# Two of 64 cache-gradient stores, issued in three parts by two queues

## The chip, the cores and the metric

The kernel runs on one core of one Trainium2 chip. The metric is device time in microseconds of one launch. A run's time is a little longer than the span of the profile, which goes from the first to the last instruction of the program.

## What is computed

The reference is one decode step of an attention block and a gated MLP that stand side by side, and its whole backward pass. Only the core of it is shown; everything is bfloat16, with a batch of 2, one query position, 32 query heads over 16 key heads, a cache of 4096 positions and a head size of 128.

```python
q = (xn @ wq) per head;  k, v = caches, each shared by 2 query heads
o = softmax(q k^T / sqrt(128)) v;  y_attention = o @ wo
h = (xn @ w_gate) * (xn @ w_up);   y_mlp = h @ w_down
out = x + y_attention + y_mlp                        # xn = layernorm(x)
_out, _vjp = jax.vjp(_f, A_x, A_k_cache, A_v_cache, A_wq, A_wo, B_w_gate, B_w_up, B_w_down)
_grads = _vjp(grad_out)
return (_out0, *[jnp.asarray(_g) for _g in _grads])
```

The two caches and their gradients make up most of the bytes. A cache has 2 x 16 slabs of 4096 x 128 elements (1 MB each), and its gradient has as many. Since there is one query position, the gradient of a slab is an outer product: of the softmax weights with the head's output gradient for V, and of the score gradients with the query for K.

## The kernel before

**Steps.** The kernel walks through 16 steps `s`. Each takes one batch entry `b` and one group `g` of two key heads, so it loads four slabs: K and V for `l` = 0 and 1. `t` = 0 stands for K and `t` = 1 for V. A slab lies in SBUF as 128 rows of 32 positions, 8192 bytes a row. A step turns the slabs with VectorE transposes (`turn`), forms scores on TensorE (`score`), the softmax, the output and the score gradients, and then the two cache gradients.

**The gradients of the caches.** GpSimd builds a block-diagonal matrix `BD` of the query or of the output gradient (`build_BD`) and copies small weight tiles `W` (`build_W`). `outer` waits for `BD` and starts a `head_outer` for each of the two heads. That one takes one of the store buffers `st`, which share sixteen 8 KB-a-row tiles called `big` with the caches and other work (at most five of them may be store buffers). It has four units of work; a unit is a pair of matmuls into PSUM and an eviction by ScalarE or VectorE into a quarter of the buffer. When all four are in, `put` stores the buffer as a slab of `out_2` or `out_3`, one transfer of 128 rows.

**The stores of weights.** MLP and projection weights have gradients too, which are stored from `big` tiles, in rows of 1 to 8 KB, and from small tiles `tl` of 64 rows of 1 KB. Of the latter, `tail_outer` writes some with a destination rearranged to `"(r q) f -> q r f"`, `q=4`, so that their leading dimension is 4: those chosen by `FEW_M`, `FEW_G` and `few`.

**Order.** All work is written as Python generators that yield what they need (an engine for so long, a buffer, an event, a transfer). A planner (`Order`) runs them against costs and priorities (`pr`, `OFF`, `PR`) at build time and emits the instructions of each engine in the order in which it picks them; on the chip each engine runs its own in that order. Semaphores come from the framework. All transfers of size are issued by SyncE on one queue, at most eight of them under way at a time: each waits for the landing of the one issued eight before. The planner is told of a transfer by `yield DMA("SP", ...)`; the line after it issues it. `put` has its instruction at line 699 in the profile.

## Time and profile before

| what | value |
|---|---|
| time, three runs | 461.71, 463.93, 466.58 us (median 463.93) |
| the profiled execution's own time | 462.65 us |
| its span | 460.7 us |
| bytes read and written in HBM | 92.48 MB each |
| SyncE's queue (q1) | 40416 packets, 184.96 MB |
| PE, DVE, ACT, POOL busy | 369.5, 365.9, 336.8, 143.4 us |
| granted TensorE clock, mean | 0.721 |

The page's names are these: PE is TensorE, PEld its weight loads, DVE VectorE, ACT ScalarE, POOL GpSimd, SP SyncE; an added `q` is an engine's sequencer, which issues transfers and waits. `big`, `tl`, `BD`, `W` are tiles, `in_..._dram` and `out_dram` tensors in HBM, and L699 is a line of the kernel. The core has 16 transfer engines. A DMA share of 1 means that all 16 have a packet under way, and a row of digits shows it in tenths over forty slices. Packets of one engine overlap by some nanoseconds, so the share can pass 1.

### The profile page before, as it was taken

How to read it: one execution, taken by the hardware profiler on the slowest of the kernel's cores; microseconds unless marked ns; L12 is line 12 of the kernel's file. 1: busy time of each engine (PE TensorE's matmuls, PEld its weight loads, DVE VectorE, ACT ScalarE, POOL GpSimd, SP SyncE). 2: the span in 40 equal slices, each digit the busy share in tenths (PEclk: the TensorE clock that was granted, in tenths of full speed). 3: DMA queues.
4: the chain of work that ended last, by engine and by line, in shares of the span. 5: the costliest groups of instructions: out<-in, count | busy, mean ns of one | idle time of the engine just before them, and what ended most of it. 6: DMA issues, size and time to landing. Idle time of an engine off the chain costs nothing.

```text
span 460.7 us, 15711 instructions
## 1 busy us (share of the span) xinstructions
PE 369.5 (80%) x6750; PEld 214.3 (47%) x6750; DVE 365.9 (79%) x708; ACT 336.8 (73%) x516; POOL 143.4 (31%) x174
## 2 busy tenths in 40 slices
PE   1688879798986786896978897877988887987994
PEld 1445456555443343554546364544444542544453
DVE  8887888896789687878887679886976987887782
ACT  4269638878986586775767859867867997897973
POOL 0740043403407341660016151050164364063000
PEclk9967676888776667757685678877567676675856
DMA  8999999999999999999999999999999999999995
GB/s 316 413 408 422 410 423 400 410 415 398 373 424 421 408 422 410 421 419 413 413 403 417 417 418 419 422 418 388 398 423 417 418 423 426 423 409 392 421 346 209
DMA packets 40494, 185.97 MB, mean 404 GB/s; under 512 B 3424, under 2 KB 12136, under 8 KB 24040
## 3 DMA queue, kind: packets, MB, share of 16 engines
q1 hardware_dynamic: 40416, 184.96, 99.0%
q8 instruction: 53, 0.87, 0.7%
q14 instruction: 17, 0.14, 0.1%
q10 hardware_dynamic: 8, 0.00, 0.0%
HBM read 92.48 MB, written 92.48 MB: 401 GB/s over the span
## 4 chain that ended last, share of the span: by engine, by line
DMA 34%; PE 30%; ACT 14%; DVE 12%; issue 5%; SPq 3%; DVEq 0%; ACTq 0%
DMA big<-in_A_v_cache_dram 15%; DMA out_dram<-big 14%; ACT big L470 12%; DVE big L466 7%; PE ps_o L1299 5%; PE ps_m L1451 4%; PE ps_o L730 4%; PE ps_m L1277 4%; DMA big<-in_A_k_cache_dram 3%; SPq L1201 2%; PE ps_o L767 2%; DVE big L472 2%; PE ps_m L895 2%; PE ps_m L681 2%; DMA ww<-in_A_wq_dram 1%
## 5 line engine op out<-in xcount | busy, mean ns | idle before, releaser
L470 ACT CAST big<-ps_o 128x1024 bf16<-128x1024 f32 (+2 forms) x309 | 278.9, 964 | 49.8 <-PE ps_o L1299 24.3
L466 DVE STREAM_TRANSPOSE big<-big 128x1024 f32<-128x1024 f32 x146 | 176.3, 1222 | 16.1 <-DMA big<-in_A_v_cache_dram 6.3
L1265 POOL TENSOR_TENSOR BD<-vr,mask 128x2048 bf16<-128x2048 bf16 x32 | 115.3, 3604 | 114.3 <-DVE vr L472 45.4
L472 DVE CAST big<-ps_o 128x1024 bf16<-128x1024 f32 (+1 forms) x69 | 73.4, 1065 | 19.4 <-PE ps_o L767 6.1
L1277 PE MATMUL ps_m<-big,W 128*32 128x128 bf16 x2048 | 59.7, 280 | 4.5 <-issue 1.7
L1242 POOL COPY W<-rep 32x16 bf16<-32x16 bf16 x128 | 24.8, 193 | 117.9 <-DVE rep L1015 102.0
L1277 PEld LDWEIGHTS <-W 128*32 128x32 bf16 x2048 | 47.2, 125 | 25.1 <-issue 23.9
L1299 PE MATMUL ps_o<-BD,dd 32*128 32x512 bf16 x256 | 46.9, 497 | 9.1 <-ACT big L470 8.1
L1299 PE MATMUL ps_o<-BD,pp 32*128 32x512 bf16 x256 | 44.6, 473 | 8.9 <-ACT big L470 7.3
L466 DVE STREAM_TRANSPOSE big<-ww 128x1152 f32<-128x1152 f32 (+1 forms) x25 | 32.9, 1318 | 2.6 <-DMA out_dram<-big 2.5
L1451 PE MATMUL ps_m<-big,pp 128*32 128x512 bf16 x256 | 28.9, 540 | 4.1 <-DVE pp L466 2.4
L1451 PE MATMUL ps_m<-big,dd 128*32 128x512 bf16 x256 | 27.8, 528 | 1.7 <-DVE dd L466 0.6
L1299 PEld LDWEIGHTS <-dd 32*128 32x128 bf16 x256 | 11.2, 98 | 26.5 <-issue 20.0
L1299 PEld LDWEIGHTS <-pp 32*128 32x128 bf16 x256 | 10.3, 95 | 28.1 <-issue 24.5
L767 PEld LDWEIGHTS <-xnr 32*128 32x128 bf16 x368 | 13.1, 114 | 14.5 <-issue 13.1
L730 PE MATMUL ps_o<-dyr,R 32*32 32x288 bf16 x256 | 17.8, 401 | 1.2 <-ACT big L470 1.1
L767 PE MATMUL ps_o<-D,xnr 32*128 32x128 bf16 x256 | 13.9, 265 | 5.7 <-ACT big L470 4.3
L730 PE MATMUL ps_o<-dyr,hb 32*32 32x288 bf16 x288 | 15.7, 328 | 2.8 <-ACT big L470 2.7
L1047 POOL COPY qr<-qd 128x256 bf16<-128x256 bf16 x8 | 3.2, 398 | 47.4 <-DVE qd L472 43.2
L895 PE MATMUL ps_m<-big,Wdy 128*128 128x128 bf16 x162 | 16.7, 285 | 0.6 <-DVE cr L1403 0.5
L895 PEld LDWEIGHTS <-Wdy 128*128 128x128 bf16 x162 | 15.1, 131 | 2.9 <-issue 2.7
L1352 ACT COPY mr<-m 1x128 f32<-1x128 f32 x16 | 4.7, 295 | 15.1 <-DVE m L1350 14.9
(210 smaller groups left out, 488.2 us busy)
## 6 DMA issues: line engine op xcount, KB each, us to landing
out_dram<-big SPq DMA_DIRECT2D x74, 1024.0 KB
big<-in_A_k_cache_dram SPq DMA_DIRECT2D x32, 1024.0 KB
big<-in_A_v_cache_dram SPq DMA_DIRECT2D x32, 1024.0 KB
out_dram<-big SPq DMA_DIRECT2D x17, 576.0 KB
ww<-in_B_w_down_dram SPq DMA_DIRECT2D x9, 576.0 KB
ww<-in_A_wo_dram SPq DMA_DIRECT2D x8, 576.0 KB
ww<-in_A_wq_dram SPq DMA_DIRECT2D x8, 512.0 KB
big<-in_B_w_gate_dram SPq DMA_DIRECT2D x4, 1024.0 KB
```

Of the source, the lines that this page charges most:

```text
L466: nc.vector.transpose(out, in_)
L470: nc.scalar.copy(out, in_)
L472: nc.vector.tensor_copy(out=out, in_=in_)
L681: nc.tensor.matmul(dp[32 * q:32 * q + 32, 0:P], lhsT=W, rhs=view(X, 0, P, xoff(q, s), [[FS, 4], [2, 32]]), start=(s == 0), stop=(s == S - 1))
L730: nc.tensor.matmul(o[32 * q:32 * q + 32, aa, 0:HD2], lhsT=view(t, 32 * q, 32, 2 * A + aa, [[4, 32]]), rhs=dyr[32 * q:32 * q + 32, k * HD2: ...
L767: nc.tensor.matmul(o[:, aa, j * P:(j + 1) * P], lhsT=xnr[32 * a:32 * a + 32, dc * P:(dc + 1) * P], rhs=rhs(a), start=True, stop=True)
L895: nc.tensor.matmul(dh, lhsT=Wdy[:, e, 2 * k:2 * k + P], rhs=view(X[:], 0, P, 64 * k + e, [[D, FC], [2, 32]]), start=(k == 0 and e == 0), s ...
L1242: nc.gpsimd.tensor_copy(view(W_t[t][w][:], 32 * a, 32, 6 + 8 * a, [[G * WW, 4], [WW, G], [1, 2]]), view(rep_t[grp[g]["qs"]][:], 32 * a, 32 ...
L1265: nc.gpsimd.tensor_tensor(BD_t[i][:], view(vr_t[v][:], 0, P, 0, [[0, 16], [1, Dh]]), view(mask16[:], 0, P, 0, [[1, 16], [0, Dh]]), ALU.mult)
L1277: nc.tensor.matmul(sc[32 * cq:32 * cq + 32, :], lhsT=view(W[:], 0, P, (be * G + l) * WW + 6 - 4 * c2 - 2 * l, [[1, 32]]), rhs=view(X[:], 0 ...
L1299: nc.tensor.matmul(o[:, k, :], lhsT=pr2[32 * c4:32 * c4 + 32, :], rhs=BD[32 * c4:32 * c4 + 32, 8 * l + 4 * h2:8 * l + 4 * h2 + 4, :], star ...
L1451: nc.tensor.matmul(ct[32 * j:32 * j + 32, :], lhsT=view(rT, 0, P, 4 * c + 2 * l, [[1, 32]]), rhs=kv_t[kvS[s][t][l]][:, Dh * c:Dh * (c + 4) ...
```

## The change

`put` gets a list `split` of row counts. For each count it issues that many leading rows as a transfer by GpSimd; the rows that remain are issued by SyncE. `head_outer` passes `SPLIT = (5, 121)` for step 4 and step 9, V, second head, and an empty list for the other 62 stores. These two stores so leave as rows 0 to 4 and 5 to 125 from GpSimd and rows 126 and 127 from SyncE. What is yielded to the planner stays the same, so the order of all other instructions does too; GpSimd's two issues stand in its program where the store was placed among GpSimd's own work.

```diff
-    def put(dst, src, nbytes, row, tag, slot, ready):
+    def put(dst, src, nbytes, row, tag, slot, ready, split=()):
         yield WAIT(*ready)
         for d, x in zip(dst, src):
             yield DMA("SP", 0.36, nbytes, row)
-            nc.sync.dma_start(d, x)
+            r0 = 0
+            for n in split:
+                nc.gpsimd.dma_start(d[r0:r0 + n], x[r0:r0 + n])
+                r0 += n
+            nc.sync.dma_start(d[r0:] if r0 else d, x[r0:] if r0 else x)
         yield ("lrel", tag, slot)
...
+    FEW_KV, SPLIT = ((4, 1, 1), (9, 1, 1)), (5, 121)
     FEW_M, FEW_G = (5, 6, 7, 8), range(3, NG)
...
-        yield SPAWN(put([oviews[t][b, G * g + l]], [st[:]], 1 << 20, 8192, "st", i, done), pr(f"out{t}", s) + PR["store"])
+        yield SPAWN(put([oviews[t][b, G * g + l]], [st[:]], 1 << 20, 8192, "st", i, done,
+                        SPLIT if (s, t, l) in FEW_KV else ()), pr(f"out{t}", s) + PR["store"])
```

## The prediction

> **What bounds the kernel now.** I read the page first, then the stretches, then the DMA queues in windows, and the chain of waits last.

> ```profile
> span 460.7 us, 15711 instructions
> DMA  8999999999999999999999999999999999999995
> q1 hardware_dynamic: 40416, 184.96, 99.0%
> ...
> 20.00:440.00 420.00, 346.92 (x6376) 199.77 (x6377) 339.25 (x608) 320.24 (x491) 136.84 (x157) 0.71 1.02 413
> 440.00:456.00 16.00, 14.00 (x232) 8.43 (x228) 9.63 (x24) 10.33 (x14) 0.00 (x0) 0.61 0.87 328
> 456.00:461.00 5.00, 0.12 (x5) 0.00 (x0) 0.34 (x1) 0.41 (x1) 0.00 (x0) 0.50 0.09 34
> ```

> The rows of the stretches give length, busy time of PE, PEld, DVE, ACT and POOL, granted clock, DMA share and GB/s. For 420 us the DMA share is 1.02 of 16 engines: packets overlap a little, and no transfer engine has a pause worth naming. PE, the busiest other engine, is at 347 of 420 us. So up to 440 us a transfer engine's own rows set the time: a row added to an engine that never rests makes that engine late by one row, and waits elsewhere cost only if they let the rings run dry. The sixteen are not equally loaded, though. The DMA view of the last microseconds, and the end of SyncE's waits:

> ```profile
> DMA  2222202020201120011111111111111111000000
> GB/s 83 83 83 83 83 0 115 0 115 0 115 0 72 40 83 26 26 51 38 51 51 51 38 51 51 51 38 51 51 51 51 38 51 51 26 13 26 26 13 0
> DMA packets 113, 0.15 MB, mean 48 GB/s; under 512 B 8, under 2 KB 100, under 8 KB 113
> ...
> DMA packets 79, 0.08 MB, mean 39 GB/s; under 512 B 4, under 2 KB 79, under 8 KB 79
> q1 hardware_dynamic: 79, 0.08, 11.2%
> ...
> out_dram<-big SPq DMA_DIRECT2D x3, 512.0 KB
> out_dram<-tl SPq DMA_DIRECT2D x26, 64.0 KB
> 456.59 0.26 SPq L1495 DMA_DIRECT2D out_dram<-xy  x1
> SPq L1597 <- DMA out_dram<-big: 2.6, 2, 1.3
> ```

> The first three rows are 456.3 to 459.5 us in slices of 0.08 us, the next two 457.55 to 459.5 us. A share of 11.2% is just under two engines of sixteen (12.5%): fourteen have finished by about 456.5 us, **two are still at it** until about 459.4 us, and SyncE ends the program waiting for their landing. What do they carry? The last big store has 512 KB in rows of 1 KB, so 32 rows for each of 16 engines. In the 1.95 us there are 79 - 4 = 75 rows of 1 KB, and two engines' shares are only 64. The other 11 come from the last 64 KB store, of which four engines take 16 rows each. So one late engine at least is among those four.

> That such stores use four engines can be counted. Each engine of a transfer ends its share with one small packet.

> ```profile
> DMA packets 40494, 185.97 MB, mean 404 GB/s; under 512 B 3424, under 2 KB 12136, under 8 KB 24040
> out_dram<-big SPq DMA_DIRECT2D x74, 1024.0 KB
> ...
> out_dram<-xy SPq DMA_DIRECT2D x2, 2.2 KB
> ...
> xy<-in_grad_out_dram ACTq DMA_DIRECT2D x1, 2.2 KB
> ```

> The list of issues (first and last row shown) adds up to 231. With 16 engines each that would be 3696 small packets; 272 are missing. In the code 18 of the 26 stores from `tl` lead with a dimension of 4, and four transfers have 2 rows: 18 x 12 + 4 x 14 = 272. So here **a transfer runs on as many engines as its leading dimension divides into, at most 16**: four for 4, two for 2.

> **The change, part by part.** The two stores are the ones that SyncE issues here:

> ```profile
> 166.70 0.33 SPq L699 DMA_DIRECT2D out_dram<-big  x1
> 289.41 0.33 SPq L699 DMA_DIRECT2D out_dram<-big  x1
> ```

> *Rows on the engines.* Now each has 128 rows of 8 KB, eight on every engine. Taken over to GpSimd's queue, the counted rule gives: 5 rows on 5 engines, one each; 121 rows on 11 engines (the largest divisor up to 16), eleven each; 2 rows from SyncE on two engines. 5 + 11 = 16, so I take the eleven to follow the five: the eleven gain 11 - 8 = 3 rows a store, 6 in all; three of the first five lose 7 a store, 14 in all; the two that SyncE's rows use lose 6, so 12. The price of a row, from a window (384 to 397 us) in which nearly only such rows move:

> ```profile
> DMA packets 762, 5.54 MB, mean 426 GB/s; under 512 B 87, under 2 KB 87, under 8 KB 87
> q1 hardware_dynamic: 761, 5.52, 101.0%
> ```

> 1.010 x 16 x 13 us = 210 us over 761 - 87 = 674 rows is 0.312 us a row with its end mark. So the eleven get +1.87 us, the relieved -3.7 to -4.4 us. No transfer of GpSimd's is in this trace. If its path kept 8 KB rows, the price is the same; from below, I see no reason for a cheaper row. If it broke them into 1 KB pieces, the window of the late engines gives 0.112 x 16 x 1.95 us / 79 = 0.044 us apiece, 0.354 us a row: 0.042 us x 22 rows, +0.9 us on each of the eleven. I take 0, nearest to the 8 KB rows, and keep 0 to +0.9 us.

> *Which late engine counts.* One of the two is among the four; it would shed 3.7 us or more. Of the other the trace says nothing, and eleven of the twelve remaining places are in the group that gains. I take it there. Its end moves by **+1.87 us**, from 459.4 to 461.3 us, and it sets the end.

> *GpSimd's time.* Four issues are added, in order with its other work, which is:

> ```profile
> 165.80 3.61 POOL L1265 TENSOR_TENSOR BD<-vr,mask 128x2048 bf16<-128x2048 bf16 x1
> 169.34 0.90 POOL L1242 COPY W<-rep 32x16 bf16<-32x16 bf16 x4
> 174.35 0.40 POOL L1047 COPY qr<-qd 128x256 bf16<-128x256 bf16 x1 [4.11 <-DVE qd L472]
> 175.84 1.84 POOL L1242 COPY W<-rep 32x16 bf16<-32x16 bf16 x8 [1.09 <-DVE rep L1015]
> ...
> 283.49 1.85 POOL L1242 COPY W<-rep 32x16 bf16<-32x16 bf16 x8 [6.74 <-DVE rep L1015]
> 299.12 3.60 POOL L1265 TENSOR_TENSOR BD<-vr,mask 128x2048 bf16<-128x2048 bf16 x1 [13.78 <-ACT vr L470]
> ```

> In program order the first pair stands behind the BD that ends at 169.41 us, the second behind the copies that end at 285.34 us. At 169.4 us the evictions of the first store are done (SyncE issued it at 166.70), so the pair waits for nothing; behind it stand four copies of W, then qr. The second pair waits to about 289.4 us, in a pause that lasts to 299.12 us. Price of an issue: not below nothing; from below by rows SyncE's 0.33 us; from above GpSimd's longest row, 3.61 us. I take 1 us, nearer to SyncE's, since a row of 126 pairs of addresses is far from the 128 x 2048 elements of a BD. Two of them, 2 us, go into the pauses of 4.11 and 13.78 us: **0** on the path. At 3.61 us each a pair takes 7.2 us; that is 3.1 us more than the first pause, and the copies, qr and what follows would be late by it.

> *SyncE.* Its issue stays, with 2 rows: between 0.26 us (the 2-row store above) and 0.33 us. Nothing is gained or lost there. Its ring has 126 rows less at that place, and GpSimd's rows come beside it on the same engines; so the loads behind don't move by more than the rows themselves do.

> *The store buffer* comes free when all three parts have landed. A 1 MB store now takes this long from issue to release, as the chain shows:

> ```profile
> 295.13 16.57 DMA out_dram<-big
> ACT big L470 <- DMA out_dram<-big: 11.6, 8, 4.0
> ```

> Eight rows are 2.5 us; the rest of 16.57 us is the ring's backlog and the late engine. GpSimd's rows don't stand behind that backlog, so eleven rows (3.4 us, twice that if they take turns with SyncE's) land no later: 0. The waits that this could touch are ACT's, 11.6 us in 8 waits over the whole span.

> **Sum.** 462.65 us of the profiled execution (span 460.7 us and 1.95 us around it) + 1.87 + 0 + 0 = **464.5 us**, +0.4%. This execution is 1.3 us below the median of the three runs, 463.93 us; against the median the sum is 465.8 us, so 464.5 us leans to the low side on purpose, since the relief of the other late engine can only pull down.

> **Rivals.**

> *Both late engines are relieved (faster).* The first four carry 18 stores of 64 KB nearly alone: 18 x 16 x 0.044 us is 12.7 us more than the other twelve have. That speaks for lateness among the first five; against it, at most two of the four are late, so their load alone doesn't make an engine late. If both late ones are there, the tail's last 1.9 us go (the xy store, issued at 456.59 us, then ends the program, by estimate 0.9 us after its issue), and loads land earlier too: the chain has

> ```profile
> 368.33 15.48 DMA big<-in_A_k_cache_dram
> ```

> which waits for the last engine. Gain 1.9 to 4.4 us, less where the eleven's +1.87 us takes over; I price it at the far end, 458.3 us.

> *GpSimd's rows are dealt out differently.* If 121 rows go eight each to fifteen engines and one to the sixteenth, and 5 rows one each to the first five, the first two engines get 2 rows a store more, three more get 1, and the last loses 7. The late engine of the four then has +2 or +4 rows, 0.6 to 1.25 us: 463.3 us. If the other late engine is the last, it loses 4.4 us, which helps nothing while the first stays. [...]

> *GpSimd's issues are the new wait (slower).* At 3.61 us an issue or more, four W copies and qr come 3.1 us late at 170 us, `PE` and `DVE` behind them, and the first store lands that much later, so ACT waits for its buffer. It decides from the point where a pair takes more than 4.1 us. For it: no row bounds the issue from above but 3.61. Against: rings are 10 us and more deep (16.57 us above), so a short stall is swallowed. With the +1.87 us and 3.6 us of such stall: 468.1 us. [...]

> *No effect:* rows dealt out as before: 462.7 us.

> **How the numbers follow.** Chances: forecast 0.36, both relieved 0.25, issues a wait 0.22, other dealing 0.15, no effect 0.02. The time is the forecast's, 464.5 us. The three runs lie within 461.71 to 466.58 us, so a measurement tells about 1% from no change. Faster by over 1%: six tenths of the second case, which is priced at 0.94% and may exceed it, and a little from the scatter: 0.17. Slower by over 1%: 0.18 of the wait's 0.22 (468.1 us is +1.2%) and 0.07 from the forecast with the 0.9 us of pieces: 0.25. Within 1%: 0.58. The likeliest case alone spans 462.7 to 467; the range takes in the prices of the rivals on both sides, 458.3 to 468.1 us, with its upper end at 469 us for the pieces on top of the wait.

> **What would show it.** A queue of GpSimd's with 252 rows, 2.06 MB. If the divisor rule holds with one end mark an engine, its small packets number 2 x (5 + 11) = 32; more speak for another dealing. Rows at 0.31 us. Each GpSimd issue near 1 us; W copies at 170 us late by at most 2 us. In the tail, one engine (6% share) instead of two, ending near 461 us. I am wrong if no engine is late after the other fifteen, if the span ends below 459 us, or if GpSimd's work or ACT's waits for store buffers grow by more than 3 us.

## The result, and the profile after

The changed kernel takes 465.06 us (median of 14 runs, 464.03 to 466.79); the kernel before takes 463.32 us (14 runs, 461.71 to 466.58). The ratio is **1.0031, interval 1.0018 to 1.0045**: 0.8 to 2.1 us more (intervals here are of 95%). Forecast were 464.5 us for the profiled execution, 0.4% over the 462.65 us before; it took 464.06. The time came out as forecast. The mechanism did not, as the experiments show. All ratios compare runs in the fast state alone, of which s112_16 and g121x_16 have two each, split_16 three and g128_16 four.

The page of the changed kernel, its span and its queues:

```profile
span 462.3 us, 15725 instructions
DMA packets 40566, 185.97 MB, mean 402 GB/s; under 512 B 3496, under 2 KB 12208, under 8 KB 24112
q1 hardware_dynamic: 40136, 182.90, 97.7%
q0 software_dynamic: 352, 2.06, 1.2%
```

GpSimd's queue, q0, moves the forecast 2.06 MB, but in 352 packets: 252 rows and 100 small packets, where 32 were forecast. So the transfers were not dealt out by the rule that I had counted from SyncE's stores.

The stretches (length, busy PE, PEld, DVE, ACT, POOL, clock, DMA share, GB/s), first the kernel before with a cut that the prediction did not show, then the changed one:

```profile
20.00:170.00 150.00, 121.42 (x2359) 72.29 (x2360) 123.12 (x219) 110.97 (x173) 49.01 (x59) 0.73 1.02 410
170.00:290.00 120.00, 99.36 (x1861) 58.74 (x1858) 97.57 (x181) 86.70 (x131) 37.83 (x53) 0.71 1.02 415
290.00:320.00 30.00, 24.25 (x521) 16.52 (x517) 23.18 (x40) 21.39 (x35) 7.21 (x2) 0.74 1.01 413
320.00:440.00 120.00, 101.89 (x1643) 52.22 (x1644) 95.38 (x171) 101.17 (x154) 42.79 (x44) 0.70 1.01 414
```

```profile
20.00:170.00 150.00, 121.08 (x2359) 72.20 (x2360) 122.65 (x218) 110.94 (x173) 48.56 (x55) 0.73 1.02 407
170.00:290.00 120.00, 98.16 (x1871) 58.18 (x1869) 97.30 (x181) 86.52 (x131) 39.75 (x59) 0.73 1.02 415
290.00:320.00 30.00, 23.88 (x511) 15.72 (x508) 23.29 (x40) 21.37 (x35) 7.62 (x3) 0.72 1.01 394
320.00:440.00 120.00, 98.20 (x1632) 49.94 (x1631) 94.00 (x167) 99.71 (x152) 42.73 (x44) 0.73 1.01 416
456.00:462.30 6.30, 2.16 (x16) 1.09 (x16) 0.94 (x5) 0.75 (x2) 0.00 (x0) 0.50 0.33 117
```

Right behind the second changed store, from 290 to 320 us, 394 instead of 413 GB/s were moved: 19 x 30 us is 0.57 MB, or 1.4 us of traffic at 413 GB/s. **The share of busy engines stayed at 1.01**: the engines show as busy, and move less. Behind the first store (170 to 290 us) nothing is missing. These are single executions, though, and they scatter: the 3 GB/s less before 170 us lie ahead of the change and make 0.45 MB, and in the kernel g128_2 below, whose time is that of the kernel before, the row of 290 to 320 us has 405 GB/s (its profiled execution was the slowest of its runs). So the row alone proves little. More can be seen in the 14 us in which GpSimd's rows of the second store move. The DMA view of 289 to 303 us, in the kernel before, in the changed one, in g128_2 (the same two stores whole, by GpSimd) and in g121x_2 (121 rows of them alone):

```profile
DMA packets 811, 5.91 MB, mean 422 GB/s; under 512 B 90, under 2 KB 90, under 8 KB 90
...
DMA packets 797, 5.58 MB, mean 399 GB/s; under 512 B 117, under 2 KB 117, under 8 KB 117
...
DMA packets 847, 5.94 MB, mean 424 GB/s; under 512 B 96, under 2 KB 128, under 8 KB 129
...
DMA packets 766, 5.52 MB, mean 394 GB/s; under 512 B 90, under 2 KB 95, under 8 KB 95
```

The two kernels with whole stores move 422 and 424 GB/s, the two with 121 rows 399 and 394. In the changed kernel 0.33 MB are missing, 0.8 us of traffic. In the last row of the stretches PE still works 2.16 us, where it had 0.12 us after 456 us before: the whole end has moved back.

How long a row of GpSimd's was on its engine, from the DMA view of two windows, 169.5 to 181.5 us and 289 to 303 us:

```profile
q0 software_dynamic: 176, 1.03, 22.3%
...
q0 software_dynamic: 176, 1.03, 22.1%
```

0.223 x 16 x 12 us is 42.8 us; less 50 small packets of 0.009 us, that is 0.336 us for each of 126 rows. In the second window, 0.221 x 16 x 14 us likewise gives 0.389 us. Forecast was 0.312 us. Together the 252 rows held their engines 3.0 + 9.7 = 12.7 us longer, 0.8 us an engine; what SyncE's rows beside them lost can't be read off these views.

GpSimd's rows in the timeline, and the tail (DMA view of 459.4 to 461.1 us):

```profile
169.52 1.23 POOL L701 DMA_DIRECT2D out_dram<-big  x2
170.74 0.92 POOL L1247 COPY W<-rep 32x16 bf16<-32x16 bf16 x4
174.54 0.40 POOL L1052 COPY qr<-qd 128x256 bf16<-128x256 bf16 x1 [2.88 <-DVE qd L472]
289.34 1.08 POOL L701 DMA_DIRECT2D out_dram<-big  x2 [4.72 <-ACT big L470]
299.91 3.60 POOL L1270 TENSOR_TENSOR BD<-vr,mask 128x2048 bf16<-128x2048 bf16 x1 [9.49 <-ACT vr L470]
...
DMA packets 68, 0.07 MB, mean 39 GB/s; under 512 B 4, under 2 KB 68, under 8 KB 68
q1 hardware_dynamic: 68, 0.07, 11.0%
```

An issue takes 0.54 to 0.62 us, and pauses of 2.88 and 9.49 us still follow. In the tail 0.110 x 16 is 1.8 engines: two are still late, not one.

### The profile page after: what moved, and what is told of

Same layout as the page of the kernel before. It is cut to its first block, busy times and chain, and to the rows that moved or that the text cites. A ratio compares the mean times of both kernels' runs of the same rounds, so it can differ in the third digit from the quotient of the medians.

```text
span 462.3 us, 15725 instructions
## 1 busy us (share of the span) xinstructions
PE 366.3 (79%) x6750; PEld 211.4 (46%) x6750; DVE 365.9 (79%) x708; ACT 336.9 (73%) x516; POOL 145.4 (31%) x178
## 2 busy tenths in 40 slices
DMA  8999999999999999999999999999999999999995
DMA packets 40566, 185.97 MB, mean 402 GB/s; under 512 B 3496, under 2 KB 12208, under 8 KB 24112
## 3 DMA queue, kind: packets, MB, share of 16 engines
q0 software_dynamic: 352, 2.06, 1.2%
## 4 chain that ended last, share of the span: by engine, by line
DMA 40%; PE 27%; DVE 13%; ACT 11%; issue 5%; SPq 3%; POOL 1%; DVEq 0%; ACTq 0%; POOLq 0%
DMA big<-in_A_v_cache_dram 21%; DMA out_dram<-big 15%; ACT big L470 8%; DVE big L466 7%; PE ps_o L1305 4%; PE ps_o L734 4%; PE ps_m L1457 4%; DMA big<-in_A_k_cache_dram 3%; DVE big L472 3%; PE ps_m L1282 3%; SPq L1206 2%; PE ps_o L771 2%; PE ps_m L681 1%; PE ps_m L900 1%; DMA ww<-in_A_wq_dram 1%
## 5 line engine op out<-in xcount | busy, mean ns | idle before, releaser
L470 ACT CAST big<-ps_o 128x1024 bf16<-128x1024 f32 (+2 forms) x309 | 279.0, 967 | 48.8 <-PE ps_o L1305 26.5
L472 DVE CAST big<-ps_o 128x1024 bf16<-128x1024 f32 (+1 forms) x69 | 73.5, 1065 | 18.5 <-PE ps_o L771 5.7
L1282 PE MATMUL ps_m<-big,W 128*32 128x128 bf16 x2048 | 56.5, 269 | 4.8 <-issue 2.4
L1282 PEld LDWEIGHTS <-W 128*32 128x32 bf16 x2048 | 45.0, 120 | 24.3 <-issue 23.0
L1305 PE MATMUL ps_o<-BD,dd 32*128 32x512 bf16 x256 | 43.7, 469 | 12.3 <-ACT big L470 9.7
L1457 PE MATMUL ps_m<-big,pp 128*32 128x512 bf16 x256 | 30.0, 559 | 4.1 <-DVE pp L466 2.4
L771 PEld LDWEIGHTS <-xnr 32*128 32x128 bf16 x368 | 13.3, 119 | 12.4 <-issue 11.5
## 6 DMA issues: line engine op xcount, KB each, us to landing
out_dram<-big SPq DMA_DIRECT2D x72, 1024.0 KB
big<-in_A_k_cache_dram SPq DMA_DIRECT2D x32, 1024.0 KB
big<-in_A_v_cache_dram SPq DMA_DIRECT2D x32, 1024.0 KB
ww<-in_A_wq_dram SPq DMA_DIRECT2D x8, 512.0 KB
big<-in_B_w_gate_dram SPq DMA_DIRECT2D x4, 1024.0 KB
```

The lines of the kernel that those rows point to most:

```text
L470: nc.scalar.copy(out, in_)
L472: nc.vector.tensor_copy(out=out, in_=in_)
L771: nc.tensor.matmul(o[:, aa, j * P:(j + 1) * P], lhsT=xnr[32 * a:32 * a + 32, dc * P:(dc + 1) * P], rhs=rhs(a), start=True, stop=True)
L1282: nc.tensor.matmul(sc[32 * cq:32 * cq + 32, :], lhsT=view(W[:], 0, P, (be * G + l) * WW + 6 - 4 * c2 - 2 * l, [[1, 32]]), rhs=view(X[:], 0 ...
L1305: nc.tensor.matmul(o[:, k, :], lhsT=pr2[32 * c4:32 * c4 + 32, :], rhs=BD[32 * c4:32 * c4 + 32, 8 * l + 4 * h2:8 * l + 4 * h2 + 4, :], star ...
L1457: nc.tensor.matmul(ct[32 * j:32 * j + 32, :], lhsT=view(rT, 0, P, 4 * c + 2 * l, [[1, 32]]), rhs=kv_t[kvS[s][t][l]][:, Dh * c:Dh * (c + 4) ...
```

## The experiments

In the diffs `put` sends the listed parts of a store one after the other, each by the engine beside it. In the kernels that only store rows, `rows(G, 121, 8)` is eight stores of 121 rows by GpSimd, and S is SyncE; the diffs show these stages shortened. All ratios are to the kernel before.

**Rows alone (m1_rows): how is a transfer dealt out?**

> This kernel does no gradient at all: it only stores rows of 8 KB from one zeroed buffer, stage by stage, with a fill of the buffer by VectorE between the stages (1 x 121 rows by GpSimd; 8 x 121 by GpSimd; 8 x 5 by GpSimd; 16 x 2 by SyncE; 121 by SyncE; 128 by SyncE; 128 by GpSimd; 4 x 121 by GpSimd beside 32 x 4 by SyncE; 16 x 5 by GpSimd beside 32 x 4 by SyncE). A row takes 0.31 us on an engine. Theory D (the divisor rule of the prediction): one transfer of 121 rows runs on eleven engines, eleven rows each: 3.4 us of packets at a share of about 0.69. Eight of them take 27 us if they always use the same eleven, 19 to 21 us if the start rotates. Theory C (the ceiling, the prediction's rival of another dealing): eight rows on fifteen engines and one on the last: 2.5 us at a share of 0.94 for one, 20 us at 0.94 for eight. The stage of 121 rows by SyncE tells whether the divisor rule holds there (3.4 us at 0.69). In the stage with 32 x 4 rows beside GpSimd's 121s, C expects the first four engines alone to be busy after about 10 us, until 20 us (32 + 32 rows). In the last stage five shared engines take 32 + 16 rows (15 us), separate ones 10 us.

```diff
+ rows(G, 121); rows(G, 121, 8); rows(G, 5, 8); rows(S, 2, 16); rows(S, 121); rows(S, 128); rows(G, 128)
+ 4 x (rows(G, 121), rows(S, 4, 8));  rows(G, 5, 16), rows(S, 4, 32)
```

The DMA view of one GpSimd store of 121 rows, of eight stores of 5, and of one of 121 by SyncE; then, from the stretches, the eight stores of 121 in full flow (share and GB/s at the end of the row):

```profile
DMA packets 144, 0.99 MB, mean 142 GB/s; under 512 B 23, under 2 KB 23, under 8 KB 23
...
DMA packets 256, 0.33 MB, mean 26 GB/s; under 512 B 216, under 2 KB 216, under 8 KB 216
...
DMA packets 132, 0.99 MB, mean 136 GB/s; under 512 B 11, under 2 KB 11, under 8 KB 11
...
22.00:34.00 12.00, 0.00 (x0) 0.00 (x0) 1.00 0.95 398
```

SyncE's 121 rows have 11 end marks: eleven engines, the divisor rule. GpSimd's have 23 small packets, 16 + 7, and five rows have 216 / 8 = 27, 16 + 11. Both fit one reading: each of 16 engines is given 121 / 16 rounded up, that is 8 places, or 1 place for five rows; 8 x 16 - 121 = 7 and 16 - 5 = 11 empty places go out as small packets; and all 16 engines post an end mark. Two stores give 2 x (23 + 27) = 100, the number of the changed kernel. The share of 0.95 in full flow is close to 15 engines of 16 (0.94). **Theory C holds by this count, D falls**: on this reading 121 rows are eight on each of fifteen engines and one on the last.

But the single store of 121 rows did not take the 2.5 us of C; its packets lasted from 4.5 to 9 us. And the last two stages, with SyncE's transfers of four rows beside GpSimd's, expected at 20 and at most 15 us, took 53.6 and 63.8. A second question came up: what makes a row dear?

**The issuer alone (g128_2).**

> The same two stores leave whole, 128 rows each, by GpSimd; SyncE issues none of them. Eight rows on each of sixteen engines, as before the change, so only the issuer and its queue differ. Theory A (the dealing of rows makes the change's +0.3%): ratio to the kernel before 1.000 +- 0.001. Theory B (GpSimd's queue beside SyncE's, or its issues, make it): the same +0.3% as the change or a little more, 1.003 to 1.004, with the loss of bytes at 290 to 320 us that the changed kernel's trace shows.

```diff
- SPLIT = (5, 121)                # by GpSimd, the rest by SyncE
+ SPLIT = ((nc.gpsimd, 128),)     # nothing by SyncE
```

GpSimd's queue in the windows used for the changed kernel, 169.5 to 181.5 us and 289 to 303 us:

```profile
q0 software_dynamic: 144, 1.05, 20.9%
...
q0 software_dynamic: 144, 1.05, 17.9%
```

Ratio 1.0005 (0.9992 to 1.0018). With two stores, GpSimd's queue, its issues and its place among SyncE's rows cost nothing that can be measured. Theory B falls. Worked out as above, a row takes 0.312 us in both windows. Packet by packet, 3 of the 256 rows in this trace take over 0.33 us, and 41 of the 252 in that of the changed kernel.

**The dealing without GpSimd (s120_2, s120_8_2), and many stores (split_16).**

> The same two stores leave in four parts by SyncE alone: 120, 5, 2 and 1 rows. By the divisor rule for SyncE that is eight rows on fifteen engines, one each on the first five, one each on the first two and one on the first: the last engine loses 16 rows in all, the first gains 6, the second 4, three more 2. That is the dealing of theory C, made without GpSimd. Theory A (the dealing makes the +0.3%): 1.002 to 1.004, +0.6 to +1.9 us. Theory B (GpSimd's queue or issues make it): 1.000 +- 0.001, plus three more SyncE issues of 0.1 to 0.3 us a store.

> The two stores leave by SyncE as 120 and 8 rows: the last engine loses 16 rows in all, the first eight get one row a store, in a transfer of its own. The kernel with 120, 5, 2 and 1 had three such transfers on the first engine, and took 4.6 us (ratio 1.010). Theory L with the most loaded engine deciding: a third of it, +1.5 us, 1.003. Theory of added rows (eight engines, 16 rows against 16): the number of the added transfers is what counts, the same +4.6 us, 1.010.

> Sixteen stores (one in each of the sixteen steps, four rows of them in place of every one of the change's two) leave as 5 and 121 rows by GpSimd and 2 by SyncE. Theory A with dealing C: the first two engines get 32 rows more (10 us), the next three 16 (5 us), the last 112 less; the program ends 5 to 10 us later, ratio 1.011 to 1.022. Theory A with dealing D (eleven engines three rows more a store): 48 rows, +15 us, 1.032. Theory B: eight times the change's +1.4 us, +11 us, 1.025, with waits at GpSimd's other work.

```diff
+ SPLIT = ((nc.sync, 120), (nc.sync, 5), (nc.sync, 2), (nc.sync, 1))   # s120_2
+ SPLIT = ((nc.sync, 120), (nc.sync, 8))                               # s120_8_2
+ FEW_KV = [(s, 1, 1) for s in range(NS)]                              # split_16, parts as in the change
```

s120_2: 1.0100 (1.0072 to 1.0127), over twice the top of theory A's range. s120_8_2: 1.0062 (1.0039 to 1.0085), neither a third of that nor the same. split_16: 1.056 (1.0525 to 1.0595), +26 us, beyond all three expectations. The dealing costs, without GpSimd too; rows at 0.31 us each can't account for it.

**Is it lone rows, or the order of partitions? (m2_mix, s112_16)**

> Again rows of 8 KB alone, no gradient, in stages of sixteen stores each: 128 rows by SyncE; 128 + 2; 128 + 5 + 2 + 1; 112 + 16; 128 with 5 by GpSimd beside; 5 and 121 by GpSimd with 2 by SyncE. The run of rows alone gave 0.31 us a row when eight stand in a row on an engine, but 0.65 us for each transfer of one row by SyncE, and about 1.3 us by GpSimd. Theory R (a row costs 0.31 us wherever it stands): 39 us, 44, 54, 39, 44 and, with ten rows on the first two engines, 49 us. Theory L (a transfer of one row on an engine costs its latency, 0.65 us from SyncE and 1.3 us from GpSimd): 39, 50, 71, 45, 60 and 64 to 70 us.

> Sixteen stores leave by SyncE as 112 and 16 rows: seven and one row on each of the sixteen engines, so that no engine gains or loses a row; each gets a transfer of one row. Theory R (a row costs 0.31 us wherever it stands): 1.000 to 1.002 (one more end mark a store, 0.03 us). Theory L (a transfer of one row costs 0.65 us or more): 0.34 us a store on every engine, +5 us, 1.01, or more where the waits of the rings add up.

```diff
+ FEW_KV = [(s, 1, 1) for s in range(NS)]; SPLIT = ((nc.sync, 112), (nc.sync, 16))
```

The six stages of m2_mix took 42, 51, 77, 68, 62 and 81 us from fill to fill. The stage with 112 + 16, the fourth, contradicts both theories: R said 39, L 45, and it took 68. In the kernel s112_16 gave 1.0413 (1.0364 to 1.0463), four times L's figure, although by the divisor rule, seven rows and one on each of sixteen, no engine has a row more.

**Where the rows come from (m3_ports).**

> Rows of 8 KB alone, no gradient: sixteen transfers each by SyncE of 1, 2, 2 (every fourth partition), 4, 4 (every fourth), 8, 8 (every fourth), 16, 16 (every fourth) and 64 rows; then single transfers by GpSimd of 121 rows from partition 5, of 121 from partition 0 and of 128, by SyncE of 120 and of 112; then stages of twelve stores of 128 rows by SyncE, and of eleven with one more by GpSimd: as 128, as 121, as 5 and 121 (with 2 by SyncE). [...] Theory L (a transfer of one row on an engine waits for its end mark, 0.65 us by SyncE): 0.65 us for all counts up to 16, whichever partitions they come from.

```diff
+ for count, step in ((1, 1), (2, 1), (2, 4), (4, 1), (4, 4), (8, 1), (8, 4), (16, 1), (16, 4), (64, 1)):
+     rows(S, count, step=step)       # partitions 0, step, 2 * step, ...
...                                   # then the single stores and the stages of twelve
```

The DMA view of three windows: two neighbours (11.5 to 23.5 us), two rows four partitions apart (25.3 to 37 us), four neighbours (38.8 to 61 us):

```profile
DMA packets 64, 0.26 MB, mean 22 GB/s; under 512 B 32, under 2 KB 32, under 8 KB 32
q1 hardware_dynamic: 64, 0.26, 10.7%
...
DMA packets 64, 0.26 MB, mean 22 GB/s; under 512 B 32, under 2 KB 32, under 8 KB 32
q1 hardware_dynamic: 64, 0.26, 5.5%
...
DMA packets 128, 0.52 MB, mean 24 GB/s; under 512 B 64, under 2 KB 64, under 8 KB 64
q1 hardware_dynamic: 128, 0.52, 22.4%
```

0.107 x 16 x 12.0 us over 32 rows is **0.64 us a row; four partitions apart, 0.055 x 16 x 11.7 over 32 is 0.32 us**; four neighbours, 0.224 x 16 x 22.2 over 64, 1.24 us. In the two stages of two rows, the rows of the slabs that are written, their number and that of the end marks (32 for 16 transfers, so two engines each) are the same: only the partitions that are read differ. Eight and sixteen neighbours took 1.25 us a row; sixty-four, four to an engine, took 0.63. Four and eight rows four partitions apart took 0.32 us as well, sixteen about 0.36. Theory L, with 0.65 us for all of these up to sixteen, falls. **In transfers of two to sixteen neighbours a row took two to four times the 0.32 us of two rows four apart**; what slows it isn't shown.

The same view for stores of GpSimd's that stand alone, 121 rows from partition 5 (198 to 205.5 us) and 128 rows (215 to 221 us), and the fills by VectorE that close the last four stages (in brackets the time that each stage's stores took):

```profile
q0 software_dynamic: 144, 0.99, 49.5%
...
q0 software_dynamic: 144, 1.05, 42.4%
...
270.01 1.76 DVE L31 MEMSET big<- 128x2048 uint32 x1 [32.20 <-DMA out_dram<-big]
303.81 1.76 DVE L31 MEMSET big<- 128x2048 uint32 x1 [32.04 <-DMA out_dram<-big]
341.03 1.76 DVE L31 MEMSET big<- 128x2048 uint32 x1 [35.45 <-DMA out_dram<-big]
377.99 1.76 DVE L31 MEMSET big<- 128x2048 uint32 x1 [35.20 <-DMA out_dram<-big]
```

0.495 x 16 x 7.5 over 121 is 0.49 us a row (from partition 0, in m1_rows, it was 0.51), 0.424 x 16 x 6 over 128 is 0.32 us. Both stores read neighbouring partitions, so I put the difference down to which of these each engine is given; that is a guess, since no view names the engine of a row. One store of 121 among eleven whole ones takes 35.45 us against 32.04 for a whole one, **3.4 us more with seven rows fewer**. 5 + 121 + 2 takes 3.2 us more than a whole store (35.20 us).

**The controls (c2_16, g128_16).**

> Sixteen stores leave by SyncE in two parts, but cut across the columns: 128 rows of 4 KB twice, instead of 112 and 16 rows of 8 KB (which gave a ratio of 1.041). [...] Theory T (one more SyncE transfer in flight takes a place among those the queue allows, so the rings hold less): as with 112 and 16, +17 to +20 us, 1.04.

> Sixteen stores leave whole by GpSimd, 128 rows each. The same sixteen, cut into 5, 121 and 2, gave a ratio of 1.056. [...] Theory P (GpSimd's queue, its issues or the waits in its program order make it): 1.03 to 1.06.

```diff
+ nc.sync.dma_start(d[:, 0:2048], x[:, 0:2048])          # c2_16: two halves of the columns
+ nc.sync.dma_start(d[:, 2048:4096], x[:, 2048:4096])
+ FEW_KV = [(s, 1, 1) for s in range(NS)]; SPLIT = ((nc.gpsimd, 128),)   # g128_16
```

c2_16: 1.0031 (1.0014 to 1.0048), where the same number of transfers as 112 and 16 rows cost 4.1%. The price of the rows alone gives as much: in the trace of the kernel before, SyncE's rows of 8 KB take 0.315 us on the mean and those of 4 KB 0.163 us, and 16 x (16 x 0.163 - 8 x 0.315) us is 1.4 us, by estimate 1.003 (sixteen rows of 4 KB an engine in place of eight of 8 KB). Theory T falls. g128_16: 1.0078 (1.0049 to 1.0107), far below P's range; theory P falls: sixteen whole stores by GpSimd do cost something, but a seventh of the 5.6% of the same stores in 5, 121 and 2.

**The 121 rows alone (g121x_2, g121x_16).**

> The two stores leave as 121 rows by GpSimd; the other 7 rows of each are not written at all. By the dealing that the run of rows alone showed, engines one to fifteen keep eight rows and the last loses seven. Theory F (the +0.3% comes from the first engines' short transfers, and relief of the last engine is worth nothing): 1.000 +- 0.001. Theory G (the last engine is one of the two late ones, and its relief is worth 1 to 4 us, hidden in the change by the first engines' loss): 0.991 to 0.998.

> Sixteen stores leave as 121 rows by GpSimd; their other 7 rows are not written. The same sixteen gave 1.056 as 5 + 121 + 2 and 1.008 as whole stores by GpSimd. [...] Theory F (it is the 5 and 2 rows, lone rows on the first engines): they are gone, and the last engine has less to do: 1.00 to 1.01.

```diff
+ SPLIT = ((nc.gpsimd, 121),)                                             # g121x_2
+ FEW_KV = [(s, 1, 1) for s in range(NS)]; SPLIT = ((nc.gpsimd, 121),)    # g121x_16
```

The 121 rows are partitions 0 to 120 here, not 5 to 125 as in the change; the other seven are not written.

g121x_2: 1.0028 (1.0010 to 1.0046), the loss of the change, though by the dealing of theory C no engine has a row more and the last has seven fewer a store. Theory G falls. F expected at most 1.001, where the interval begins, and the interval overlaps that of g128_2 (0.9992 to 1.0018), so the question was put again with sixteen stores: g121x_16 is at 1.0432 (1.0394 to 1.0470), where F expected at most 1.01. Theory F falls: the first engines' short transfers are not there, and the loss is. Of the 4.8 points that split_16 stands above g128_16, 3.5 are the 121 rows alone. The remaining 1.3 belong to the 5 and 2, or to where the 121 begin.

The pages of g128_16 and g121x_16 show where the time went:

```profile
span 461.4 us, 15733 instructions
q1 hardware_dynamic: 38112, 168.18, 90.3%
q0 software_dynamic: 2304, 16.78, 8.7%
...
span 474.3 us, 15733 instructions
q1 hardware_dynamic: 38112, 168.18, 89.3%
q0 software_dynamic: 2304, 15.86, 8.9%
```

The two shares times the span are 456.8 and 465.8 us, the time that the packets of one engine took on the mean; the kernel before has 0.990 x 460.7 = 456.1 us. So 9.7 of the 13.6 us by which g121x_16's span is longer than that of the kernel before are **packets that took longer**, with fewer rows to move. With two stores this sum is below the scatter of single executions: 457.2 us in the changed kernel, 458.9 in g128_2.

GpSimd's rows in g121x_2, same windows as for the changed kernel:

```profile
q0 software_dynamic: 144, 0.99, 19.9%
...
q0 software_dynamic: 143, 0.99, 20.1%
```

0.199 x 16 x 12, less 23 small packets, is 0.314 us for each of 121 rows at 170 us, and 0.201 x 16 x 14, likewise, 0.373 us for each of the 120 shown at 290 us. As in the changed kernel, the second store is the dear one.

## Why the prediction was right in time and wrong in its reason

- **What bounds the kernel: right.** The share of the engines is 1.01 to 1.02 up to 440 us in both kernels. But I read it as "no pause", and took from it that only added rows cost. A full share can hide a loss in bytes: with 121 rows, 399 instead of 422 GB/s went through from 289 to 303 us, and in m3_ports the same 32 rows made a share of 5.5 or of 10.7%.
- **Rows on the engines: the step that failed.** I carried SyncE's divisor rule over to GpSimd's queue. The small packets (23 for 121 rows, 27 for five; m1_rows) fit the dealing of my rival of another dealing, eight rows on fifteen engines and one on the last. The +1.87 us of six more rows on eleven engines does not exist.
- **The price of a row: the second failure, which gave nearly the same sum.** "If its path kept 8 KB rows, the price is the same": it kept them, and they took 0.336 and 0.389 us. I priced a row by its length and its engine, and left out which partitions are read beside each other (0.32 us four apart, 0.64 and 1.24 us for two and four neighbours; m3_ports). The extra 0.8 us an engine and, by estimate, up to as much again for the rows of SyncE's that they met, is 0.8 to 1.6 us; measured are 0.8 to 2.1. That +1.87 lies beside it is chance.
- **Which late engine counts: wrong.** There are still two late engines in the tail, at 459.4 to 461.1 us, and the whole end came later: SyncE issues the store of `xy` at 459.33 us, where it was 456.59.
- **GpSimd's time, SyncE, the store buffer: right, all 0.** Two issues took 1.23 and 1.08 us, the W copies came 1.4 us late (170.74 against 169.34 us), and two whole stores by GpSimd gave 1.0005. ACT's waits for store buffers went from 11.6 to 9.3 us.
- **The rivals.** Relief of a late engine: by theory C's dealing the last one shed 14 rows in g121x_2, and nothing came of it; whether the two late engines' own relief would pay was not tried. The other dealing: it fits the small packets as a dealing, but its price, the first engines' extra rows, is not what costs (g121x_2). The issues as a wait: no (g128_2). No effect: no, the whole interval lies above 1.

What stays open: what slows rows of neighbouring partitions, which of them each engine is given, why the second store suffers and the first hardly does, and why sixteen stores cost 1.6 us each where two cost 0.7. That the 121 rows make the loss is shown with sixteen stores, and that rows of neighbouring partitions can be dear is shown with rows alone; for the two stores of the change it rests on the longer rows in its trace and on intervals that part narrowly. None of the kernels tried beats the kernel before.

## What to carry to other kernels

Before cutting a transfer, ask not only how many rows each engine gets, but from which partitions: sixteen stores cut into two halves of the columns, which left all 128 partitions in both transfers, cost 0.3% (c2_16); cut between rows they cost 4 to 6% (s112_16, split_16). A share of busy transfer engines near 1 does not say that they move what they can (422 and 399 GB/s here, both at a share of about 1); read GB/s beside it, and divide a queue's share by its rows to get the price of one. To learn how a queue deals out a transfer, count its small packets in a kernel that does nothing else.
